# GpSimd's instructions in written order, and a block's loads issued behind its rstd, eight blocks ahead in place of six

## The chip, the cores and the metric

The kernel runs on one core of a Trainium2 chip. The core has TensorE (PE in the profile, with its weight loads as PEld), VectorE (DVE), ScalarE (ACT), GpSimd (POOL) and SyncE (SP), and 16 DMA engines that move data between HBM and the on-chip memories. The metric is the device time of one execution in microseconds.

## The reference

Attention over a sliding window with a linear distance bias, then a layer norm and an MLP with a residual. In and out are float32.

```
B, H, S, D = 8, 8, 576, 64;  window = 128
scores = q @ k^T / sqrt(D) - slope[h] * (i - j)     # only 0 <= i - j < window
x = (softmax(scores) @ v), heads side by side       # B x S x 512
mu, var = mean(x), mean((x - mu)^2)                 # per row
xn = (x - mu) / sqrt(var + 1e-6) * g_ln
out = x + relu(xn @ w_ch1) @ w_ch2                  # 512 -> 2048 -> 512
```

## The kernel before

The 8 batches are taken in 4 pairs p. A pair is 9 blocks of 128 rows: blocks 0 to 7 are four 128-row stretches of each of the two batches in turn (block blk is stretch blk // 2 of batch blk % 2), and block 8 (named T) is the 64 rows that are left of each batch, put together. So there are 36 blocks, numbered n in `order`. For block n the work is:

- **loads** (`load_qk` L213, `load_v` L244, issued on GpSimd's queue, converting float32 to float16): q and k come with every even block, for both batches of the pair, v with every block. The list `loads` holds them in the order of the blocks, with the MLP's weights behind blocks 3 and 5; `place[n]` is the place in the list behind block n's v; `load_until` (L266) issues all that is not issued yet up to a place. There are four buffers for q, four for k (`raw_pool`, L86) and ten for v (`NV`, L29).
- **turn**: q and k are transposed, for pairs 0 to 2 by TensorE through PSUM (L301) with copies by VectorE and ScalarE (L333 to L338), for pair 3 by DMA transposes on SyncE's queue. `turn_at` (L684) sets it some four or five blocks ahead.
- **scores** (L436), exponentials by ScalarE (L445), **masks** by VectorE (L456), **values** in two halves (L489 on TensorE; L497 and L498 on VectorE write x). Block n reads its own keys and those of block n - 2; the T block reads those of blocks 6, 7 and 8 of its pair.
- the norm. For n below 8: `centre` and a transpose by TensorE, with the variance's root computed on VectorE. For n from 8 on: `stats` (L538), that is two VectorE instructions (L586, L587 write moments) and two small GpSimd instructions (L541 adds epsilon, L544 takes the power -0.5: rstd), and then `normal` (L524): VectorE writes xc from x, moments and rstd (L528), and SyncE's queue transposes xc to xT by DMA (L536).

The blocks are put into groups, six of 2 and then six of 4. A group goes through the MLP when all of its xT are there: `mlp1` (L732 on TensorE, evicted at L748 by ScalarE mostly) and `mlp2` (L765, or `fast_mlp2` with L831 and L849 for the groups of 4), with the sum's last step and the residual on VectorE (L909 or L849) and the store on SyncE's queue.

The order of the work is written out by hand: `steps` is a list of small steps of the attention and the norm, and `weave_at` runs them at given places between the MLP's units. For TensorE, SyncE, ScalarE and VectorE the order of the program text is the order on the engine (`manual_schedule`, L950 and L951). GpSimd is not among them: the tool that builds the program puts its instructions in order by a plan of its own. Each engine runs its instructions in order, and each waits for the data or the free buffer that it needs. So a load that waits for a buffer, or is simply being issued, holds back the rstd behind it on GpSimd.

From block 8 on, the steps of a block are: masks and values of n with `load_until` in front, and scores of n + 2; then masks of the blocks ahead and `stats(n)`; then the turns; then `normal(n)`. At n = 11 (`HURRIED`) the norm of block 11 comes right behind its stats.

Of the kernel before, what the change touches and what calls it, by code (L numbers as in the profile page):

```python
# [27 lines left out]

NV = 10  # L29
BY_DMA_TURN = 3  # L30
AHEAD = 6

FIRST_GROUPS, FIRST = 2, 4

BY_DMA = SEEN = 8
# [24 lines left out]
def kernel(  # L60
# [149 lines left out]
    def by_dma(p):  # L210
        return p >= BY_DMA_TURN
# [44 lines left out]
    loads, place = [], []  # L256
# [363 lines left out]
    for g, size in enumerate(GROUPS):  # L620
        n = sum(GROUPS[:g])
# [3 lines left out]
    count = len(order)  # L625

    def turn_step(n, *how):
        p, blk = order[n]
        return [(turn, p, blk // 2) + how]

    def scores_step(n):
        return [(scores,) + order[n]]

    def values_steps(n):
        p, blk = order[n]
        ahead = place[min(n + AHEAD, count - 1)]
        return [
            [(load_until, ahead), (masks, p, blk), (values, p, blk, 0)],
            [(values, p, blk, 1), (centre, p, blk)],
        ]  # L640

    def x_step(n, copy=nc.vector.tensor_copy):
# [6 lines left out]
    def masks_of(n, *halves):  # L649
        return [(masks,) + order[n] + halves]  # L650

    def warm_step(n):
        return [[(warm, n)]]


    steps = warm_step(11) + [[(turn_first,)]] + warm_step(3)
    steps += [scores_step(0), scores_step(1) + masks_of(0) + masks_of(1)] + warm_step(6)
    steps += values_steps(0)
    steps += warm_step(2) + [turn_step(2, True, (nc.scalar.copy, nc.scalar.copy))]
    steps += values_steps(1) + warm_step(4)  # L660
    steps += [x_step(0, nc.scalar.copy)] + warm_step(2) + [scores_step(2)]
    steps += [masks_of(2, 1) + x_step(1) + scores_step(3), values_steps(2)[0]]
    steps += [masks_of(2)]
    first = len(steps)
# [19 lines left out]
    def turn_at(n):  # L684
        ahead = [m for m in (n + 3, n + 4) if m < count and order[m][1] % 2 == 0]
        return [
            f
            for m in ahead
            if by_dma(order[m][0]) == (m == n + 4)
            for f in turn_step(m, True)  # L690
        ]

    steps.append(turn_at(8))
    for n in range(8, count):
        first_half, second_half = values_steps(n)
        step = first_half + second_half[:1]
        if n + 1 < count and order[n + 1][1] == T:
            step += [(scores_tail, order[n][0])]
        if n + 2 < count:
            step += scores_step(n + 2)  # L700
        steps.append(step)
        to_mask = [m for t in (n + 1, n + 2) if t < count for m in masks_of(t)]
        turns = [turn_at(n + 1)] if n + 1 < count else []
        if n == HURRIED:
            steps += [[(normal, n - 1)], to_mask + [(stats, n)], [(normal, n)], *turns]
        else:
            steps += [to_mask + [(stats, n)], *turns]
            if n != HURRIED - 1:
                steps.append([(normal, n)])
    combined = combine_w2()  # L710
# [2 lines left out]
    def advance_to(n):  # L713
        nonlocal done
        while done < min(n, len(steps)):
            for f, *args in steps[done]:
                f(*args)
            done += 1
# [4 lines left out]
    def mlp1(g, on_dve=()):  # L723
        xT = turned_x[g]
        w = w1 if g < FIRST_GROUPS else w1g
        cols = len(members[g]) * P
        ht = hidden[g] = hidden_pool.tile([P, NFB, 4 * P], FP16, tag="ht", name="ht")
        turn_about = chain(*zip(range(QF), range(QF, NFB)))
        for u, fb in enumerate(turn_about if g >= FAST else range(NFB)):
            ps = psum("ps_m1")  # L730
            for kb in range(NKB):
                nc.tensor.matmul(  # L732
                    ps[:, 0:cols],
                    w[:, kb, fb * P : (fb + 1) * P],
                    xT[:, kb, 0:cols],
                    start=(kb == 0),
                    stop=(kb == NKB - 1),
                )
            if u in on_dve:
                nc.vector.tensor_scalar(  # L740
                    out=ht[:, fb, 0:cols],
                    in0=ps[:, 0:cols],
                    scalar1=0.0,
                    scalar2=None,
                    op0=ALU.max,
                )
            else:
                nc.scalar.activation(  # L748
                    out=ht[:, fb, 0:cols], in_=ps[:, 0:cols], func=AF.Relu
                )  # L750
            yield cols
            if g >= FAST and u == 10:
                for i in range(4):
                    combine_hidden(g, 0, i)

    def mlp2(g, parts=((0, NFB),)):

        ht = hidden[g]
        sums = {}
        for first, end in parts:  # L760
            for at, (p, blk) in enumerate(members[g]):
                if first == 0:
                    sums[at] = ps_mm.tile([P, DM], FP32, tag="mm", name="ps_m2")
                for fb in range(first, end):
                    nc.tensor.matmul(  # L765
                        sums[at],
                        ht[:, fb, at * P : (at + 1) * P],
                        w2[:, fb, :],
                        start=(fb == 0),
                        stop=(fb == NFB - 1),  # L770
                    )
                    if fb % 4 == 3 and fb < NFB - 1:
                        yield DM
                if end == NFB:
                    finish(p, blk, sums[at])
                    yield DM
# [155 lines left out]
    def weave_at(units, *places, also=()):  # L932
        for u, _ in enumerate(units):
            advance_to(done + places.count(u))
            if u in also:
                next(combined, None)
# [10 lines left out]
    decay(m_tail, 4)  # L947
    load_until(place[3])
    engine = mybir.EngineType
    with tc.manual_schedule(engines={engine.PE, engine.SP}):  # L950
        with tc.manual_schedule(engines={engine.Activation, engine.DVE}):  # L951
            advance_to(first)
            weave_at(mlp1(0, (0, 1)), 2, 7, 8, 9, 13)
            weave_at(mlp1(1), 2, 8, 12)
            weave_at(mlp2(0, ((0, 8), (8, 12), (12, NFB))), 0, 1, 3, 4, 4, 5)
            weave_at(mlp2(1), 0, 1, 2, 3, 4, 6, 6)
            weave_at(mlp1(2), 0, 3, 3, 6, 8, 11)
            weave_at(mlp2(2), 0, 2, 4, 6, 7)


            weave_at(mlp1(3, (9, 10, 11)), 8, 8, 12, 15)
            weave_at(mlp2(3), 0, 1, 1, 3, 4, 4, 6, 6)
            weave_at(mlp1(4), 0, 4, 8, 10, 10, 14)
            weave_at(mlp2(4), 0, 2, 2, 5, 5, 7, also=(1, 4, 6))
            weave_at(mlp1(5), 0, 5, 5, 8, 10, 12, also=(3, 6, 9))
            weave_at(mlp2(5), 0, 1, 2, 4, 6, 7)
            ring += [ps_mm.tile([P, DM], FP32, tag="mm", name="ps_r") for _ in range(4)]
            for g in range(6, len(GROUPS)):
                weave_at(
                    mlp1(g), 0, 2, 5, 7, 8, 10, 13, 15, also=(1, 4) if g == 6 else ()  # L970
                )
                weave_at(fast_mlp2(g), 1, 3, 6, 7, 7, 10, 12, 13)
# [31 lines left out]
```

## Time and profile before

| | |
|---|---|
| median of the runs | 318.75 us (316.97, 318.75, 320.42) |
| the profiled execution | 317.64 us, of which the span of the program's instructions is 315.8 us |
| TensorE busy | 304.8 us (97% of the span) |
| VectorE busy | 228.8 us (72%) |
| ScalarE busy | 179.7 us (57%) |
| GpSimd busy | 125.8 us (40%), 198 instructions |
| TensorE clock granted | 0.996 of full |
| loads q, k, v | 128 DMAs on GpSimd's queue, of 128 or 64 KB each; 3.9 to 6.5 us from issue to landing in the medians of their kinds |
| xT transposes | 28 DMAs on SyncE's queue; 2.4, 3.2, 6.8 us to landing (least, median, most) |

Times on the chip's records are counted from the start of the span. A row of a timeline gives the start, the length (several instructions of one kind may stand in one row, with their count), the engine, the line of the kernel, the operation, what is written and read, and in brackets how long the engine was idle before and what ended that. The table by stage gives the busy time of each engine in a stretch of time, in the order PE, PEld, DVE, ACT, POOL, then the granted TensorE clock, the DMA share and the GB/s. In the chain that ended last each row is one link: what the end of the program waited for, followed back.

### The profile page before, as it was taken

The page shows a single profiled execution, that of the slowest core. Times are in us where ns is not written, and L with a number is a line of the kernel's source. Part 1 is how long each engine was busy: PE and PEld are TensorE (multiplying, and loading weights), DVE is VectorE, ACT ScalarE, POOL GpSimd, SP SyncE. Part 2 cuts the span into 40 slices and gives each one's busy share as a digit, 9 for nine tenths or more (in the row PEclk, how much of TensorE's full clock was granted, in tenths as well). Part 3 has the DMA queues.
Part 4 walks back from the last instruction along what each step waited for, and adds up shares of the span by engine and source line. Part 5 has one row for each costly group of instructions (what it writes and reads, how often), then busy time and mean ns, then how long its engine had stood idle before and what let it go on. Part 6 is the DMA issues. An engine that isn't in the chain of part 4 may idle for free.

```text
span 315.8 us, 9932 instructions
## 1 busy us (share of the span) xinstructions
PE 304.8 (97%) x4195; PEld 205.2 (65%) x4195; DVE 228.8 (72%) x547; ACT 179.7 (57%) x311; POOL 125.8 (40%) x198
## 2 busy tenths in 40 slices
PE   8989999999999999999999999999999999999994
PEld 2468655756757567554885488558756875784583
DVE  2788877877578698758994889479948994761363
ACT  6588765667667557378348832772487247305600
POOL 8932758666254356575254672140001001100001
PEclk9999999999999999999999999999999999999998
DMA  9999999999997999599959995892457144015004
GB/s 111 172 206 198 191 141 179 198 134 144 105 119 96 91 114 141 60 166 46 69 63 166 159 119 69 133 153 52 94 97 114 18 85 85 19 37 114 0 2 134
DMA packets 121087, 34.68 MB, mean 110 GB/s; under 512 B 112049, under 2 KB 116657, under 8 KB 121042
## 3 DMA queue, kind: packets, MB, share of 16 engines
q0 software_dynamic: 89280, 18.49, 74.1%
q1 hardware_dynamic: 31362, 15.09, 25.0%
q8 instruction: 33, 0.54, 0.7%
q10 hardware_dynamic: 400, 0.46, 0.5%
q14 instruction: 12, 0.10, 0.1%
HBM read 36.90 MB, written 9.44 MB: 147 GB/s over the span
## 4 chain that ended last, share of the span: by engine, by line
PE 84%; DVE 6%; ACT 4%; issue 2%; DMA 1%; POOL 1%; DVEq 0%; ACTq 0%
PE ps_r L732 27%; PE ps_r L831 23%; PE ps_m L732 10%; PE ps_m L765 9%; PE ps_sc L436 4%; PE ps_sc L301 3%; PE ps_r L489 3%; PE ps_warm L283 2%; PE ps_pv L489 2%; ACT probs L445 2%; DMA q<-in_q_dram 1%; DVE x L498 1%; DVE o L909 1%; DVE probs L456 1%; DVE o L849 1%
## 5 line engine op out<-in xcount | busy, mean ns | idle before, releaser
L732 PEld LDWEIGHTS <-w1g 128*128 128x128 f16 x640 | 60.4, 98 | 50.1 <-issue 1.9
L732 PE MATMUL ps_r<-xT,w1g 128*128 128x512 f16 x384 | 85.1, 379 | 0.0
L445 ACT ACTIVATE probs<-ps_sc 128x1024 f16<-128x1024 f32 x56 | 54.2, 1026 | 51.1 <-PE ps_sc L436 51.1
L748 ACT ACTIVATE ht<-ps_r 128x512 f16<-128x512 f32 x96 | 56.2, 600 | 31.6 <-PE ps_r L732 31.5
L541 POOL TENSOR_TENSOR rstd<-moments,powers 128x1 f32<-128x1 f32 x28 | 6.9, 245 | 99.1 <-DVE moments L587 98.1
L765 PE MATMUL ps_m<-w,ht 128*128 128x512 f16 x192 | 46.0, 380 | 0.0
L247 POOL DMA_DIRECT2D vx<-in_v_dram x40 | 34.5, 876 | 26.3 <-PE ps_r L489 9.0
L831 PE MATMUL ps_r<-w,ht 128*128 128x256 f16 x384 | 44.1, 273 | 0.0
L456 DVE TENSOR_TENSOR probs<-probs,m 128x1024 f16<-128x1024 f16 x56 | 37.5, 688 | 7.2 <-ACT probs L445 7.0
L831 PEld LDWEIGHTS <-ht 128*128 128x128 f16 x384 | 37.1, 98 | 4.8
L748 ACT ACTIVATE ht<-ps_m 128x256 f16<-128x256 f32 x91 | 33.3, 390 | 8.8 <-PE ps_m L732 6.2
L732 PE MATMUL ps_m<-xT,w1g 128*128 128x256 f16 x256 | 31.3, 273 | 1.9 <-DVE o L909 0.7
L765 PEld LDWEIGHTS <-ht 128*128 128x128 f16 x192 | 17.0, 98 | 17.5
L237 POOL DMA_DIRECT2D q<-in_q_dram x30 | 20.6, 693 | 16.0 <-PE ps_sc L301 8.6
L586 DVE BATCH_NORM_STATS2 st<-x 128x6 f32<-128x512 f16 x36 | 24.7, 685 | 0.0
L237 POOL DMA_DIRECT2D k<-in_k_dram x30 | 20.1, 681 | 5.6 <-DMA w<-in_moe_w_ch_dram 3.0
L436 PE MATMUL ps_sc<-q,k 64*64 64x128 f16 (+1 forms) x1088 | 20.7, 209 | 1.5 <-ACT probs L445 1.0
L831 PE MATMUL ps_r<-w,hs 128*128 128x256 f16 x192 | 21.9, 273 | 0.0
L489 PEld LDWEIGHTS <-probs 128*128 128x128 f16 x448 | 18.8, 97 | 4.7 <-DVE probs L456 0.3
L831 PEld LDWEIGHTS <-hs 128*128 128x128 f16 x192 | 18.8, 98 | 2.2
L849 DVE TENSOR_TENSOR o<-ps_r,o 128x512 f32<-128x512 f32 (+1 forms) x25 | 16.1, 655 | 5.0 <-PE ps_r L831 4.9
L528 DVE TENSOR_SCALAR xc<-x,moments,rstd 128x512 f16<-128x512 f16 x28 | 12.0, 428 | 10.4 <-POOL rstd L544 10.3
(89 smaller groups left out, 386.1 us busy)
## 6 DMA issues: line engine op xcount, KB each, us to landing
out_dram<-o SPq DMA_DIRECT2D x66, 128.0 KB, 2.5
k<-in_k_dram POOLq DMA_DIRECT2D x32, 128.0 KB, 6.0
vx<-in_v_dram POOLq DMA_DIRECT2D x32, 128.0 KB, 6.5
w<-in_moe_w_ch_dram POOLq DMA_DIRECT2D x8, 512.0 KB, 10.9
q<-in_q_dram POOLq DMA_DIRECT2D x24, 128.0 KB, 5.0
q<-in_q_dram POOLq DMA_DIRECT2D x24, 64.0 KB, 3.9
k<-in_k_dram POOLq DMA_DIRECT2D x8, 64.0 KB, 4.9
vx<-in_v_dram POOLq DMA_DIRECT2D x8, 64.0 KB, 6.3
```

Of the source, the lines that this page charges most:

```text
L237: nc.gpsimd.dma_start(out=t[b * n // 2 : (b + 1) * n // 2], in_=src[2 * p + b, :, i * P : i * P + n, :].rearrange("h (c r) d -> c h r d", ...
L247: nc.gpsimd.dma_start(out=vx[p0 : p0 + n, :, 0:D], in_=v[b, :, t0 : t0 + n, :].rearrange("h p d -> p h d"),)
L436: nc.tensor.matmul(in_halves(ps[cols, j, n, t, :])[:, r, queries], kt[rows, hp, cols], in_halves(qt[rows, b, hp])[:, r, queries], start=Tr ...
L445: nc.scalar.activation(out=dst.rearrange("p (n j) q -> p j n q", j=2), in_=ps.rearrange("p j n t q -> p j n (t q)"), func=AF.Exp, scale=in ...
L456: nc.vector.tensor_tensor(out=dst, in0=dst, in1=mask, op=ALU.mult)
L489: nc.tensor.matmul(ps[:, i, :], pr[:, h, t, :], vext[(p * NSLOT + o) % NV][:, h, :], start=(n == 0), stop=(n == len(terms) - 1),)
L586: nc.vector.bn_stats(out=st, in_=xs[order[n]])
L732: nc.tensor.matmul(ps[:, 0:cols], w[:, kb, fb * P : (fb + 1) * P], xT[:, kb, 0:cols], start=(kb == 0), stop=(kb == NKB - 1),)
L748: nc.scalar.activation(out=ht[:, fb, 0:cols], in_=ps[:, 0:cols], func=AF.Relu)
L765: nc.tensor.matmul(sums[at], ht[:, fb, at * P : (at + 1) * P], w2[:, fb, :], start=(fb == 0), stop=(fb == NFB - 1),)
L831: nc.tensor.matmul(banks[name][pair][:, pair, :], lhs[:, fb, pair * P : (pair + 1) * P], rhs[:, fb, :], start=(first and fb == 0 and (pair ...
L849: nc.vector.tensor_tensor(out=o[:, at, cols], in0=banks[name][at.start][:, at, :], in1=(x if to_x else o)[:, at, cols], op=ALU.add,)
```

## The change

Three things are edited. GpSimd joins the engines whose order is the written one. `AHEAD` goes from 6 to 8, so that the loads of block n + 8, not n + 6, are issued in block n's steps. And those loads stand in another place: for n below 8 behind the second half of values and `centre`, in place of in front of the first half; from n = 8 on behind `stats(n)`, in place of in front of the masks and values of block n.

```
-AHEAD = 6
+AHEAD = 8
...
+    def load_step(n):
+        return [(load_until, place[min(n + AHEAD, count - 1)])]
+
     def values_steps(n):
         p, blk = order[n]
-        ahead = place[min(n + AHEAD, count - 1)]
         return [
-            [(load_until, ahead), (masks, p, blk), (values, p, blk, 0)],
-            [(values, p, blk, 1), (centre, p, blk)],
+            [(masks, p, blk), (values, p, blk, 0)],
+            [(values, p, blk, 1), (centre, p, blk)] + load_step(n) * (n < BY_DMA),
         ]
...
         to_mask = [m for t in (n + 1, n + 2) if t < count for m in masks_of(t)]
+        stats_step = [(stats, n)] + load_step(n)
         turns = [turn_at(n + 1)] if n + 1 < count else []
         if n == HURRIED:
-            steps += [[(normal, n - 1)], to_mask + [(stats, n)], [(normal, n)], *turns]
+            steps += [[(normal, n - 1)], to_mask + stats_step, [(normal, n)], *turns]
         else:
-            steps += [to_mask + [(stats, n)], *turns]
+            steps += [to_mask + stats_step, *turns]
...
-    with tc.manual_schedule(engines={engine.PE, engine.SP}):
+    with tc.manual_schedule(engines={engine.PE, engine.SP, engine.Pool}):
```

`BY_DMA` is 8: the blocks from 8 on have their x transposed by DMA. Nothing that is computed, and no number of instructions or DMAs, changes by the text.

## The prediction

> **What bounds the kernel now.** I read the busy times first, then the busy times by stage, and then the places where TensorE really stands still.
>
> ```profile
> span 315.8 us, 9932 instructions
> ## 1 busy us (share of the span) xinstructions
> PE 304.8 (97%) x4195; PEld 205.2 (65%) x4195; DVE 228.8 (72%) x547; ACT 179.7 (57%) x311; POOL 125.8 (40%) x198
> ```
>
> TensorE is busy for 304.8 of 315.8 us and GpSimd for 40%. A change on GpSimd can only pay where GpSimd makes TensorE wait. The busy times by stage (length, then PE's busy time and count, then the other engines) say where that can be:
>
> ```profile
> 60.00:80.00 20.00, 19.00 (x373) 12.92 (x371) 14.31 (x41) 13.39 (x27) 14.13 (x20) 1.00 1.78 152
> 80.00:135.00 55.00, 53.08 (x954) 35.67 (x952) 42.78 (x101) 33.79 (x64) 26.51 (x46) 1.00 1.00 103
> 135.00:285.00 150.00, 150.00 (x1824) 103.30 (x1823) 116.09 (x249) 80.42 (x118) 44.89 (x75) 1.00 0.84 92
> 285.00:310.00 25.00, 25.00 (x169) 16.33 (x167) 9.96 (x16) 9.55 (x16) 0.00 (x0) 1.00 0.16 35
> ```
>
> From 135 to 310 us TensorE has no idle time at all. It idles 1.92 us between 80 and 135 and 1.00 us between 60 and 80. Before 80 us GpSimd computes no rstd and only loads, each load in the order of the list, so the written order is nearly the old one there. All there is to win is therefore some 2.9 us. The chain that ended last shows GpSimd as a link in one place only (start, length, what):
>
> ```profile
> 85.96 0.76 PE ps_sc L301 x64
> ...
> 88.14 0.68 POOL k L237
> 88.82 0.22 POOL rstd L541
> ...
> 89.66 0.60 POOL rstd L544
> ...
> 90.28 0.06 DVE xc L528
> ...
> 94.57 0.42 DVE x L498
> ...
> 95.86 0.67 DVE o L909
> ```
>
> Around it the timelines of VectorE and of TensorE say how long the two engines waited (in brackets, with what ended it):
>
> ```profile
> 87.27 0.18 DVE L587 BATCH_NORM_AGGREGATE moments<-st 128x2 f32<-128x6 f32 x1
> 90.28 0.41 DVE L528 TENSOR_SCALAR xc<-x,moments,rstd 128x512 f16<-128x512 f16 x1 [1.89 <-POOL rstd L544]
> ```
>
> ```profile
> 93.83 0.60 PE L732 MATMUL ps_m<-xT,w1g 128*128 128x256 f16 x4
> 95.05 1.16 PE L732 MATMUL ps_m<-xT,w1g 128*128 128x256 f16 x8 [0.63 <-DVE x L498]
> 96.58 2.56 PE L732 MATMUL ps_m<-xT,w1g 128*128 128x256 f16 x22 [0.37 <-DVE o L909]
> ```
>
> Block 9's moments were ready at 87.45. Its rstd stood behind the loads of q and k of block 20 and ended at 90.25; VectorE stood still for 1.89 us, and VectorE is what TensorE then waits for (it has to empty a PSUM bank).
>
> **What is late now.** I set the end of each moments (L587) against the start of its rstd (L541). Of 28 blocks, 25 start within 0.1 us. Three are late because a load is being issued: block 8 by 1.07 us (79.06 to 80.13), block 9 by 1.37 (87.45 to 88.82) and block 17 by 2.06 (137.21 to 139.27, behind 7.7 us of loads). Block 8's lateness is hidden: VectorE reaches its xc at 82.06, with no idle time before it. Block 17's costs VectorE 1.84 us at 140.23, where TensorE never idles, so nothing. Block 9's is the one that counts.
>
> **Part 1: the rstd goes ahead of the loads.** With the two loads out of the way, block 9's rstd starts 0.09 us after the moments, like the other 25, and its two steps end 0.83 us later (94.56 to 95.38 for block 10): 88.38. VectorE is busy with a copy until 88.40, so xc goes from 90.28 to about 88.43, which is 1.85 us earlier. What is late next? The first o (L909) needs a sum that TensorE ends at 88.5, so it follows at 88.8. The x of block 11 need matmuls that end at 92.50, so they go from 94.57 and 95.12 to about 92.9 and 93.5. TensorE wants their banks at 94.43: both are then free. The second o needs TensorE's 93.8, runs to about 95.0, and frees its bank before TensorE's 95.3. So both waits fall. TensorE took 96.58 - 93.83 = 2.75 us for 4 + 8 matmuls that cost 0.109 us each in the row of 22 ((2.56 - 0.16) / 22, with 0.16 us for the last one's drain), that is 1.31. The loss is 1.44 us. I take **-1.4**; the bounds are 0 (another wait takes its place) and -2.9 (all idle time of the two stages).
>
> **Part 2: each block's loads behind its rstd.** The loads are the same in number and size, one block issued per block. A GpSimd load costs 0.57 to 0.95 us of its queue, so a block costs 0.9 us (v alone), 3.7 (q x2, k x2, v; 100.06 to 103.72), 3.8 to 4.3 (a pair's last block) or 5.5 (pair 3: 163.24 to 168.64). The next rstd is queued behind them. The time from one rstd's end to the next moments is 5 to 7 us nearly everywhere. The tight places are block 18's loads between rstd 10 and 11 (95.38 to 98.55 = 3.2 us, against 3.7) and the 5.5 us of blocks 27 and 31 (5.3 us). The first is up to 0.5 us late where VectorE already waits 0.94 us (xc at 99.48): **0 to +0.5**, and I take 0, since rstd 10 moves further ahead than the moments of 11 do. In the other two VectorE has 1.7 and 0.8 us of other work before its xc: 0.
>
> Beside that, xc now nearly always runs while a load is being issued. Its 22 runs without one beside them average 409 ns, its 6 with one 499 ns (longest 648). For blocks 8 to 16 that is 9 x 0.09 = 0.8 us on VectorE at most, in a stage where VectorE idles 12.2 of 55 us. I take **+0.1**; the bounds are 0 and 9 x 0.24 = 2.1. The Trainium skill, "Advanced Engine Details and Errata", section "VectorE Performance Modes", speaks against the change here: the second port of VectorE is shared with GpSimd, and the two block each other. The mean of 499 against 409 agrees with it in sign, but three of the six runs are at 397 to 450, which a strict block would not leave.
>
> **Part 3: eight ahead in place of six.** It sounds like more, but the old order ran further than six: v of block 20 went out at 102.81, between the rstds of 11 and 12. With ten buffers, v of n+8 takes the buffer that values(n) reads last, and stats(n) comes after values(n), so the new load finds it free. q and k of n+8 replace a buffer turned four blocks earlier. Loads now come later, but not too late: q of block 27 moves from 131.67 to about 157.1, lands at most 7.3 us after its issue (the longest of that stage), at about 168 for the last of the seven, and is turned on SyncE's queue at 172.75. Block 29: issued from 170.4, turned at 197.5. Block 35: issued from 219.1, turned at 238.78. Cost **0**; if one of these covers were gone, the xT issued behind it on SyncE's queue would be late too.
>
> **Sum:** -1.4 + 0.1 = -1.3. The profiled execution took 317.64 us (span 315.8): 316.3. The median of the runs, 318.75, lies 1.1 above it, so the forecast for a median is **317.4**. The three runs spread over 316.97 to 320.42, so 1% (3.2 us) is about what a measurement can tell from no change.
>
> **Rivals.**
> 1. *More than one stall goes.* With loads spread out, the waits near 73, 104, 115 and 123 us shrink too. Against it: the chain has ScalarE at 104 and 123. It gives at most -2.9: 315.8; some luck in the runs makes it over 1%.
> 2. *Given back on VectorE.* The slower xc, at 0.15 to 0.24 us in nine blocks, takes 1.4 to 2.1 us, which is the whole gain: 318.7. By the skill's rule on the shared port, taken strictly, it would be this. For it: 648 and 600 ns in two of six. Against it: VectorE's idle time in that stage.
> 3. *A late rstd elsewhere.* Now the loads of n+8 stand before rstd n+1. Block 11's is late by 0.5 us and VectorE's chain carries half of block 9's gain away: 318.1.
> 4. *Slower: xT lands behind the loads.* xT(n) (L536) is now issued just as the loads of n+8 start. Its landing takes 3.2 us in the median, but 6.8 us for block 20, where seven loads were issued beside it. mlp1 of a four-block group starts 7.86 us (group 7), 6.93 (8) and 6.76 (9) after its last xT was issued, and group 4 would have 93.8 - 88.9 = 4.9. It decides from a landing of about 6.8 us on. At 8 us the four lose 0.1 + 1.1 + 1.2 + 3.1 = 5.5 us: 318.75 - 1.4 + 5.5 = 322.9. Against it: for blocks 14, 18 and 22, with loads beside them, it took 4.7, 6.4 and 5.1. The Trainium skill, "DMA: Bandwidth & Descriptors", section "Queues, rings and completion order", says that each DMA engine takes turns between queues packet by packet. By that rule, an estimate, xT would take about twice its shortest 2.4 us, 4.8, and this rival would not exist; the 6.8 us do not fit it.
> 5. *It doesn't do what it says.* That the order is not followed would show as loads between a moments and its rstd; time as before, 318.75.
>
> **Chances.** Forecast 0.55, rival 1 0.13, rival 2 0.10, rival 3 0.09, rival 4 0.10, rival 5 0.03. Over 1% faster (below 315.6) needs rival 1 or a lucky median: 0.15. Over 1% slower (above 321.9) is rival 4 and little else: 0.11. Within 1%: 0.74. The range of 315.0 to 320.6 takes in rivals 1, 2, 3 and 5 and about 2 us of the runs' spread, and leaves rival 4 out.
>
> **What would show it.** Right: all rstd start within 0.1 us of their moments up to block 10; the 1.89 us before the xc of block 9 are gone, and with them TensorE's 0.63 and 0.37; TensorE busy about 54.2 of the 55 us from 80 to 135; loads end near 225 us, not 212. Wrong: TensorE idle after 135 us at the first L732 of a group (rival 4), xc near 600 ns throughout (2), a new wait for rstd at block 11 (3). The forecast falls if DMA landings, which the old order spread over more time, are the real limit.

## The result, and the profile after

The median of ten runs is 315.73 us (314.93 to 316.73), beside 317.67 us (316.97 to 320.42) for the kernel before, now also over ten runs. The ratio is 0.9931, with an interval of 0.9909 to 0.9954: faster by 0.7%, within the 1% that the prediction held likeliest. The forecast for the median was 317.4 us; the gain was forecast at 1.3 us and is 1.9 us. In a second comparison on another occasion the medians were 315.83 and 317.22 us, a gain of 1.4 us (ratio 0.9944, 0.9914 to 0.9975).

The profiled execution took 314.93 us. Its span and busy times, from the page of the kernel after:

```profile
span 313.1 us, 9910 instructions
## 1 busy us (share of the span) xinstructions
PE 303.6 (97%) x4195; PEld 205.2 (66%) x4195; DVE 227.8 (73%) x547; ACT 179.4 (57%) x311; POOL 126.8 (41%) x198
```

The busy times by stage of the kernel after (the columns are those of before):

```profile
60.00:80.00 20.00, 19.66 (x375) 13.60 (x373) 14.24 (x40) 13.77 (x27) 7.17 (x11) 1.00 1.14 117
80.00:135.00 55.00, 54.10 (x956) 36.12 (x954) 44.80 (x105) 35.11 (x65) 27.89 (x47) 1.00 1.00 107
135.00:285.00 150.00, 150.00 (x1824) 103.18 (x1822) 114.30 (x246) 79.47 (x118) 51.01 (x83) 1.00 0.94 97
```

TensorE's idle time between 80 and 135 us has fallen from 1.92 to 0.90 us, and that between 60 and 80 from 1.00 to 0.34. GpSimd's work has moved out of the stage before 80 us (14.13 to 7.17) into the one after 135 (44.89 to 51.01), as later loads must. Around block 9, the timelines of GpSimd, of VectorE and of TensorE of the kernel after (its MLP lines have numbers that are 3 higher, so L732 is L735 now):

```profile
86.42 0.18 POOL L541 TENSOR_TENSOR rstd<-moments,powers 128x1 f32<-128x1 f32 x1 [6.26 <-DVE moments L587]
86.67 0.56 POOL L544 TENSOR_TENSOR rstd<-rstd,powers 128x1 f32<-128x1 f32 x1
87.19 1.21 POOL L237 DMA_DIRECT2D q<-in_q_dram  x2
```

```profile
86.14 0.18 DVE L587 BATCH_NORM_AGGREGATE moments<-st 128x2 f32<-128x6 f32 x1
...
87.27 0.41 DVE L528 TENSOR_SCALAR xc<-x,moments,rstd 128x512 f16<-128x512 f16 x1
```

```profile
92.65 4.09 PE L735 MATMUL ps_m<-xT,w1g 128*128 128x256 f16 x36
```

The rstd now waits for its moments and the loads come behind it. xc starts 1.13 us after its moments began, where it was 3.01, with no idle time in front. The three rows of TensorE from before (4, 8 and 22 matmuls with idle times of 0.63 and 0.37 us before the second and the third; the third row goes on to 24 behind the end of that view) are one row of 36. Both waits are gone.

**Where the 2.7 us between the two profiled executions come from.** TensorE's instructions stand in the same order in all kernels of this case. So I read, in each trace, the start of the same instructions: the first transposes of each `turn` (L301). The intervals between three of them, in us:

```
kernel                 the turn at 72.6 to     the turn at 86.0 to     the turn at 99.3 to
                       the one at 86.0         the one at 99.3         the last (176.7)
before                 13.33                   13.33                   77.45
after                  12.73                   11.84                   77.41
```

Block 9 lies in the middle interval: **-1.49 us**. The other large difference, 0.60 us, lies in the first interval. Up to 72.6 us the two differ by 0.53 us. From 99.3 us on they run alike. The experiments say which of these belong to the change.

### The profile page after: what moved, and what is told of

Read it like the earlier page. It is cut to its first block, busy times and chain, and to the rows that moved or that the text cites. A ratio compares the mean times of both kernels' runs of the same rounds, so it can differ in the third digit from the quotient of the medians.

```text
span 313.1 us, 9910 instructions
## 1 busy us (share of the span) xinstructions
PE 303.6 (97%) x4195; PEld 205.2 (66%) x4195; DVE 227.8 (73%) x547; ACT 179.4 (57%) x311; POOL 126.8 (41%) x198
## 4 chain that ended last, share of the span: by engine, by line
PE 87%; DVE 4%; ACT 3%; DMA 1%; issue 1%; POOL 1%; DVEq 0%; ACTq 0%; POOLq 0%
PE ps_r L735 27%; PE ps_r L834 23%; PE ps_m L768 13%; PE ps_m L735 10%; PE ps_sc L436 5%; PE ps_sc L301 3%; PE ps_r L489 3%; PE ps_pv L489 2%; DMA k<-in_k_dram 1%; ACT probs L445 1%; DVE o L852 1%; ACT k L334 1%; PE ps_tx L581 1%; PE ps_tr L301 1%; ACT q L333 1%
## 5 line engine op out<-in xcount | busy, mean ns | idle before, releaser
L735 PEld LDWEIGHTS <-w1g 128*128 128x128 f16 x640 | 60.6, 98 | 48.4 <-issue 1.4
L735 PE MATMUL ps_r<-xT,w1g 128*128 128x512 f16 x384 | 85.1, 380 | 0.0
L735 PE MATMUL ps_m<-xT,w1g 128*128 128x256 f16 x256 | 30.9, 273 | 0.9 <-ACT ht L751 0.6
L497 DVE RECIPROCAL rec<-ps_r 128x4 f32<-128x4 f32 x36 | 6.3, 175 | 19.6 <-PE ps_r L489 19.6
```

Of the source, the lines that this page charges most:

```text
L735: nc.tensor.matmul(ps[:, 0:cols], w[:, kb, fb * P : (fb + 1) * P], xT[:, kb, 0:cols], start=(kb == 0), stop=(kb == NKB - 1),)
```

## The experiments

**The one lateness put back.** The changed kernel, with block 18's loads in front of block 9's rstd. As `load_until` issues all that stands before them in the list, block 17's six loads come ahead of that rstd too:

```
-        stats_step = [(stats, n)] + load_step(n)
+        stats_step = load_step(n + 1) * (n == 9) + [(stats, n)] + load_step(n)
```

> The changed kernel with one thing put back: the loads of block 18 (q twice, k twice, v) are issued before block 9's rstd, not behind block 10's. Theory A (the gain is block 9's rstd, which no longer stands behind loads): the loads of blocks 16, 17 and 18 now fill GpSimd's queue from the end of rstd 8 (78.8 us) for some 8.4 us, so rstd 9 starts 1 to 2 us after its moments, VectorE idles again before xc of block 9, TensorE's two waits near 93 us come back, and 1.4 to 1.8 us of the gain go: ratio to before about 0.998, and 0.5 us remain from elsewhere. Theory B (the gain is that the loads are spread over more time and everything lands in quieter DMA queues): the loads are still spread as in the changed kernel, ratio 0.993 as there.

Measured: 316.15 us beside 317.13, ratio 0.9968 (0.9948 to 0.9988). rstd 9 starts 1.04 us after its moments, and the middle interval is 12.49 us, so 0.65 of the 1.49 us are gone. The timelines of VectorE and of TensorE in this run:

```profile
89.08 0.41 DVE L528 TENSOR_SCALAR xc<-x,moments,rstd 128x512 f16<-128x512 f16 x1 [1.04 <-POOL rstd L544]
```

```profile
94.04 4.12 PE L735 MATMUL ps_m<-xT,w1g 128*128 128x256 f16 x36 [0.47 <-DMA xT<-xc]
```

VectorE waits for rstd again, as theory A has it. But TensorE does not wait for a bank this time. It waits for xT of block 9, which was issued at 89.52 with loads in flight, until 94.04. So theory A holds in kind and was too high in size: 1.4 to 1.8 us were expected to go and 0.65 went (the expected ratio of 0.998 still lies inside the interval). The lateness reached TensorE by another way than in the kernel before. Whether that comes from its being smaller or from the eleven loads that now run right ahead of it, this run does not separate. Theory B would have left 0.993, which lies just outside the interval, and the middle interval speaks against it.

**GpSimd's written order alone.** The kernel before, with only the last line of the diff (`AHEAD` 6, loads in front of the masks):

```
-    with tc.manual_schedule(engines={engine.PE, engine.SP}):
+    with tc.manual_schedule(engines={engine.PE, engine.SP, engine.Pool}):
```

> The kernel before with GpSimd in written order alone: the loads stay in front of the masks, six blocks ahead. On GpSimd this is nearly the changed kernel's order: block n+7's loads come behind rstd n. Theory A: the whole gain, ratio 0.993 (0.991 to 0.995), with rstd 9 within 0.1 us of its moments; rstd 11 still late by some 0.5 us, since six loads stand before it. Theory C (the place behind rstd and the eight blocks bring a part of their own): clearly less gain, ratio 0.996 or more.

Measured: 315.55 us beside 317.13, ratio 0.9951 (0.9930 to 0.9972). The middle interval is 11.84 us, exactly that of the whole change, rstd 9 starts 0.09 us after its moments, and rstd 11 is 0.49 us late. TensorE's timeline has the one row of 36 matmuls, with no wait in it:

```profile
93.07 4.09 PE L732 MATMUL ps_m<-xT,w1g 128*128 128x256 f16 x36
```

The ratio lies between what the two theories expected and its interval holds both, so it does not decide between them. The trace does: the written order brings the whole of block 9's gain.

**The place and the eight blocks alone.** The changed kernel without that line.

> The changed kernel with GpSimd left out of the written order: the loads stand behind rstd and eight blocks ahead in the text, and the building tool orders GpSimd's queue. In the built program GpSimd's order is then the same, instruction for instruction, as before the change. Theory A (only the order on the queue counts): ratio 1.000, rstd 9 again 1.4 us late, TensorE's waits at 94 and 96 us and the pause near 73 us back. Theory C (the place in the text or the distance acts by itself): some of the gain, 0.998 or less.

Measured: 317.49 us beside 317.22, ratio 1.0005 (0.9971 to 1.0039): no change. Its timelines of VectorE and of TensorE show the old stall again:

```profile
89.62 0.41 DVE L528 TENSOR_SCALAR xc<-x,moments,rstd 128x512 f16<-128x512 f16 x1 [1.88 <-POOL rstd L544]
```

```profile
93.12 0.60 PE L735 MATMUL ps_m<-xT,w1g 128*128 128x256 f16 x4
94.40 1.16 PE L735 MATMUL ps_m<-xT,w1g 128*128 128x256 f16 x8 [0.68 <-DVE x L498]
95.92 2.78 PE L735 MATMUL ps_m<-xT,w1g 128*128 128x256 f16 x24 [0.37 <-DVE o L912]
```

The middle interval is 13.33 us, as before to the hundredth. One thing is not as expected: the pause near 73 us is not back, although the instructions of every engine, not only of GpSimd, stand in the order of the kernel before (waits on semaphores left aside). TensorE's timeline there, first of the kernel before, then of this one:

```profile
72.63 0.54 PE L301 MATMUL ps_sc<-iden,q 64*64 64x64 f16 x14
73.58 0.34 PE L301 MATMUL ps_sc<-iden,q 64*64 64x64 f16 x18 [0.41 <-issue]
```

```profile
72.58 0.69 PE L301 MATMUL ps_sc<-iden,q 64*64 64x64 f16 x32
```

In one the 32 transposes break off after 14 of them for 0.41 us, in the other they run through. The first interval is 12.72 us here and 13.33 in the kernel before. So those 0.60 us belong to one profiled execution and not to the change. All ten traces of this case say where such differences arise: from the start of the next 32 transposes (those of k) to the turn at 86.0 each has 12.22 us. Only the 32 of q in front of them differ: 0.50 or 0.51 us in six of the traces, 1.10 in the kernel before.

**Loads put back beside that pause.** The changed kernel, with q and k of block 17 issued at once behind block 15's loads (`load_tail` issues them and takes them out of the list):

```
-        return [(load_until, place[min(n + AHEAD, count - 1)])]
+        return [(lambda: load_until(place[min(n + AHEAD, count - 1)]),)] + [(load_tail, 1)] * (n == 7)
```

> The changed kernel with q and k of block 17 (four loads) issued at once behind block 15's, so that they run near 69 to 72 us, as they did before the change; nothing else moves before 100 us but that rstd 9 has fewer loads around it. All runs in written order so far lost a pause of 0.6 us at 73 us, in the middle of TensorE's transposes, where no semaphore explains it. Theory E (the pause comes from loads that are in flight then, for instance because TensorE's instructions are fetched late beside them): the pause of 0.4 us or more is back and the ratio is 0.995. Theory F (the pause is chance, or belongs to the other loads of that time, q, k and v of blocks 16 and 18): no pause, ratio 0.993.

Measured: 315.61 us beside 317.22, ratio 0.9933 (0.9901 to 0.9964). The four loads run at 69.5 to 71.9 us, as intended. The first interval is 12.97 us, 0.24 more than in the changed kernel, and all of it lies in the same 32 transposes (0.75 us against 0.51), but there is no pause of 0.4 us. Theory E is not borne out, and the next run shows that such a difference comes without these loads too. What stopped TensorE for 0.41 us in the one execution stays open.

**The changed kernel once more.**

> The changed kernel once more, beside the others on the same chip, so that its stages can be set against theirs: ratio 0.993, no pause near 73 us, rstd 9 within 0.1 us and rstd 11 0.47 us late. If the pause near 73 us is chance, it may be there this time.

Measured: 315.83 us beside 317.22, ratio 0.9944 (0.9914 to 0.9975). The middle interval is 11.84 us again; the first is 13.02, where it was 12.73, again in the 32 transposes alone (0.80 us against 0.51). Executions of one program differ by 0.3 us there. The 0.53 us up to that turn do not belong to the change either: it starts at 72.63 us in the kernel before, and in the two executions of the changed kernel at 72.10 and at 72.74.

**Six blocks ahead in place of eight.** The changed kernel with `AHEAD = 6`.

> The changed kernel with the loads six blocks ahead in place of eight. Theory A: rstd 9 is as early as with eight, so ratio 0.993; and rstd 11 has only one load (v) before it, so it is not 0.47 us late and up to 0.35 us more are gained: 0.992. Theory D (eight blocks are needed, the loads would come too late at six): q and k of block 15 are issued behind rstd 9 at about 87 us, land at about 96 and are turned at 96.7; if they are late TensorE waits there by 1 us or more and the ratio is 0.996 or more; SyncE's transposes of pair 3 start later by 5 us, which TensorE should not see.

Measured: 315.15 us beside 317.13, ratio 0.9927 (0.9900 to 0.9953). The middle interval is 11.86 us, and rstd 11 starts 0.09 us after its moments. The transposes of block 27 by DMA are issued at 172.58 us, where they were at 170.00 with eight blocks, and TensorE does not see it. Theory D falls: six would do. The rest of the expectation falls too, but the middle interval cannot show it: the xc of block 11 comes behind its end (in the changed kernel at 96.99, where the interval ends at 96.67). From there to the next turn (the one at 110.9 in the kernel before) every trace has 11.61 us, with rstd 11 in time or late. So rstd 11 in time gains nothing. (This run is 0.2 us shorter than the changed kernel further on, before the turn at 117.9; the run with loads put back beside the pause, in which rstd 11 is late, is so too.)

**Block 18's loads behind rstd 11.** The changed kernel with one load step left out, so that the next one issues both blocks:

```
-        stats_step = [(stats, n)] + load_step(n)
+        stats_step = [(stats, n)] + load_step(n) * (n != HURRIED - 1)
```

> The changed kernel with the loads of block 18 moved from behind rstd 10 to behind rstd 11. Theory A: rstd 11, which starts 0.47 us after its moments in the changed kernel, starts within 0.1 us, VectorE's idle time before the xc of block 11 falls from 1.37 to 0.95 us, and TensorE gains 0.3 to 0.4 us: ratio 0.992, which these rounds can just tell from 0.993. If VectorE's wait there is hidden: 0.993.

Measured: 315.10 us beside 317.13, ratio 0.9927 (0.9899 to 0.9955), with 11.61 us behind the middle interval, as everywhere: no gain that these runs can tell. VectorE's timeline, first of the changed kernel, then of this one:

```profile
96.99 0.41 DVE L528 TENSOR_SCALAR xc<-x,moments,rstd 128x512 f16<-128x512 f16 x1 [1.37 <-POOL rstd L544]
```

```profile
96.81 0.41 DVE L528 TENSOR_SCALAR xc<-x,moments,rstd 128x512 f16<-128x512 f16 x1 [0.93 <-POOL rstd L544]
97.69 0.42 DVE L333 COPY q<-ps_sc 128x512 f16<-128x512 f16 x1 [0.46 <-PE ps_sc L301]
```

rstd is earlier, VectorE's wait for it is 0.44 us shorter, and VectorE then waits 0.46 us for TensorE's transposes. In the changed kernel that second wait is not there. The lateness of rstd 11 was hidden behind TensorE's transposes.

**More loads behind a group's last block.** The changed kernel with two loads of 128 KB into buffers that nothing reads, behind the loads of blocks 15, 19, 23 and 27 in the steps:

```
+        return step + [(load_extra, n)] * (n in (15, 19, 23, 27))
```

> The changed kernel with two more loads of 128 KB, into buffers that nothing reads, behind the loads of blocks 15, 19, 23 and 27: behind rstd of the last block of each four-block group, whose xT the group's first matmuls wait for. Theory G (rival 4 of the prediction: xT lands behind the loads, and the cover is nearly used up at 6.8 us): xT of blocks 19, 23 and 27 lands over 6.8 us after its issue and TensorE waits at the first matmuls of groups 7, 8 and 9, by up to 1.5 us each: ratio 0.996 to 1.005. Theory H (the transposes get their turn beside whatever number of loads): landing as in the changed kernel, 4 to 6.6 us, no wait, ratio 0.993.

Measured: 316.03 us beside 317.22, ratio 0.9950 (0.9920 to 0.9981), not to be told from the changed kernel. xT of blocks 19 and 23 landed 4.9 and 4.1 us after its issue, and no group's first matmuls waited. The run tests less than it should: the extra loads stand behind five and more microseconds of ordinary ones, so they were issued only 4.2 us after those transposes. Behind block 15 they were issued 0.45 us after its transpose: xT landed in 5.8 us there, against 4.5 in the changed kernel, and the 8.37 us until its group starts covered that. So theory G is not tested where its cover is short, and it stays open whether more loads there would make a group wait. What the run did delay is the next rstd: those of blocks 20, 24 and 28 started 1.87, 1.86 and 0.86 us after their moments. VectorE idled 0.10 and 1.02 us for the first two, and TensorE was busy for 149.94 of the 150 us from 135 to 285. An rstd that is 1.9 us late there is nearly free, like block 17's in the kernel before.

## Why the prediction was right, step by step

- **What bounds it**: right. TensorE is bound everywhere but in a few places, the gain lies in one of them, and from 135 us on nothing changed. One reading was wrong: in the kernel before the loads up to 80 us do not stand in the order of the list. The queue had q and k of blocks 17 and 18 ahead of v of block 16. In the kernel after all loads are in the list's order, and GpSimd's busy time from 60 to 80 us is half of what it was. TensorE did not gain by it: the 12.22 us up to the turn at 86.0 are the same in all traces.
- **Block 9's rstd, -1.4 us**: right, with 1.49 us in the middle interval, and shown from both sides (0.65 us of it given back in the run that makes the rstd 1.04 us late; all of it missing where GpSimd's order stayed). xc moved by 1.88 us against 1.85 forecast. One way was missing from the step: in that run the late rstd reached TensorE through xT of block 9 and not through a bank.
- **Block 11's rstd, 0 to +0.5, taken as 0**: the size is right, the reason wrong, so this term came out by luck. I said that rstd 10 moves further ahead than the moments of 11 do. It did not: the time between them is 3.20 us, where it was 3.17. The rstd was 0.47 us late, as rival 3 had it, and VectorE's wait before xc of block 11 grew from 0.94 to 1.37 us; TensorE's transposes hide it, and nothing of block 9's gain is lost. The loads of blocks 27 and 31 made rstd 20 and 24 late by 0.14 and 0.12 us, of the order of the 0.2 us by which 5.5 us of loads exceed the 5.3 us there.
- **xc beside a load, +0.1**: 17 of the 28 xc now run beside one, with a mean of 431 ns (longest 619) against 408 ns for the others, where I had 499 against 409. Two of the 17, with 582 and 619 ns, make all of the difference; the other 15 took 396 to 414 ns, like an xc without a load. The stages after 99.3 us run as before, so no cost can be seen. The Trainium skill, "Advanced Engine Details and Errata", section "VectorE Performance Modes", lets VectorE's two-port work and GpSimd's block each other; with 15 of 17 xc unchanged, rival 2, which took that rule strictly, is out. Whether the port is what slowed the other two is not shown.
- **Eight blocks, cost 0**: right. The last load is issued at 219.9 us (206.7 before) and lands at 223.5, against a forecast of loads ending near 225. The run with six blocks shows that the number does nothing that these runs can tell, and the run without GpSimd's written order that the place in the text does nothing by itself.
- **Rival 1** (more than one stall goes) looked true in the two profiles, since TensorE's idle time between 60 and 80 us fell by 0.66. It is not: 0.60 us of it is the pause that one execution happened to have, and behind 99.3 us, where the other waits lie that it names, the two kernels run alike. That the median of 315.73 us falls on this rival's 315.8 is chance: it comes mostly from the base, which lay 1.1 us lower over ten runs.
- **Rival 4** (xT behind the loads): the landings did lengthen, and the groups did not wait. The median went from 3.2 to 4.6 us (the line of the view of xT stands below; the traces hold a landing for 21 of the 28 transposes before, and for 22 after). What decides is the last block of a group: xT of blocks 19 and 23 landed in 5.9 and 4.1 us, and their groups start 7.8 and 6.9 us after its issue; for block 27, with 6.7 us, the trace holds no landing, and TensorE did not wait. The longest landing, 6.6 us, is block 16's, which ends no group, and in the second execution of the changed kernel one took 7.0 us (block 11, whose group starts 14.4 us after its issue). So the cover held, with 1.9 us or more to spare for blocks 19 and 23. Its mechanism is real in one place: in the run with rstd 9 late behind eleven loads, TensorE waited 0.47 us for xT of block 9. The Trainium skill, "DMA: Bandwidth & Descriptors", section "Queues, rings and completion order", has each DMA engine take turns between the queues; the estimate of 4.8 us from it meets the new median, but not the landings of 6.5 and 6.6 us.
- **The sum**: -1.3 forecast. The traces give -1.49, and the medians -1.9 and -1.4 in the two comparisons. The absolute forecast of 317.4 was 1.7 us too high. 1.1 us of this is the base: the three runs shown had a median of 318.75, and ten have 317.67.

The landings of xT, from the view of that tile of the kernel after:

```profile
DMA to landing us min/median/max: 2.4/4.6/6.6
```

## What to carry to other kernels

A small instruction that a critical engine waits for should not stand behind bulk issues on its queue. Look first where that engine's wait reaches the bound: of three late rstd only one cost TensorE anything, and one of 0.47 us in the kernel after, and two of 1.9 us in the run with more loads, were all but free. When a building tool orders a queue, moving a line in the text may change nothing, so compare the order that was built. And before the difference of two single profiles is read as the change's work, set the same instructions of both against each other, and of a third execution too.

## What the hardware showed that I had not expected

TensorE stopped for 0.41 us in the middle of 32 transposes in one execution of the kernel before, with no wait in the records, and did not in another program with the same order of instructions on every engine. Two executions of the changed kernel differed by 0.3 us in the same 32 transposes, and from the next ones on to the turn at 86.0 all ten traces agree to the hundredth (12.22 us). And with GpSimd's loads moved next to xT's transposes on the other queue, the median landing was 1.4 us longer (4.6 against 3.2), without any stage after 99.3 us getting longer.
